# One queue for all transfers of the loop: loads, delayed stores and transposes issued by SyncE in a windowed-attention backward kernel

## The chip, the cores and the metric

The kernel runs on one core of one Trainium2 chip. The metric is device time in microseconds (us) of one execution. Five engines carry the work: TensorE (PE; its weight loads are shown as PEld), VectorE (DVE), ScalarE (ACT), GpSimd (POOL) and SyncE (SP). Transfers are issued by an engine's instruction stream and then carried out by the core's 16 DMA engines. In the profile, an issuing stream is shown as SPq, POOLq or ACTq.

## The reference

Forward and backward of attention in windows of 8 x 8 pixels over a 256 x 256 image with 384 channels, all in bf16:

```python
H = W = 256; C, win = 384, 8          # x and grad_out: (1, 256, 256, 384)
def forward(x, wqkv, wo):
    xw = windows_of(x)                 # 1024 windows, each 64 pixels x 384
    q, k, v = split(xw @ wqkv)         # wqkv: (384, 1152)
    p = softmax(einsum('bqc,bkc->bqk', q, k) * C ** -0.5)
    return image_of(einsum('bqk,bkc->bqc', p, v) @ wo)
out, vjp = jax.vjp(forward, x, wqkv, wo)
return out, *vjp(grad_out)             # out_0 = out, out_1 = dx, out_2 = dwqkv, out_3 = dwo
```

## The kernel before

**Tiling.** Two windows (128 pixels) make a pair of partition halves, and four pairs stacked in the image make a quad: 128 partitions x 4 x 384. The image is 128 quads. The kernel works with products of the weights (A from the q and k weights, B from the v and output weights) made once at the start, so a quad needs the transposed x and the transposed output gradient, their projections, scores, a softmax and its gradient, and sums for the weight gradients.

**The loop.** The loop at the end of the kernel runs i from -1 to 128. Each turn calls `step(c, b, a, ahead)`, which works on three quads in different stages: `a` = quad i+1 (projections), `b` = quad i (scores, softmax and the u and v products), `c` = quad i-1 (`attend`: the products with the probabilities, the outputs and dx). `filler` puts the weight-gradient sums of earlier quads, in groups of three, between these parts.

**Order.** The order in which instructions stand on each engine is written out by hand (`tc.manual_schedule` with all five engines). The framework only adds the semaphore waits. Each engine's stream runs in that order, and a waiting instruction holds back all that stands behind it.

**Transfers of one turn**, in the order in which SP's stream holds them:

1. `load_turn(sts[i + 2])`: two transposing transfers, dT<-dq and xT<-xq of quad i+2 (line 134), 12 blocks of 128 x 128 each.
2. `turn(b)`: PS<-ps of quad i (line 239), 4 blocks; it follows the last softmax step.
3. `load(ahead)`: four copies of x for quad i+3 (line 126), 96 KB each.
4. `to_tokens(a)`: tok<-zy of quad i+1 (line 171), 24 blocks; it follows the second `gather`.

POOL's stream holds four copies of the output gradient (dq, line 127) from `load`, and nine stores of the quad in `attend` (lines 298 to 305): four of 96 KB to out_0, three of 96 KB and two of 48 KB to out_1. Each store of `attend` stands right behind the evictions that make its data. The evicted outputs lie in tiles "o" and "d" of a pool with 8 buffers each, and a quad uses 4 of each.

**Consumers.** dT is first needed by `project(a, 0, ...)` of the following turn (pj<-dT, line 145), xT by `project(a, 1, ...)` of the same turn. PS is needed by `attend` of the following turn, and tok by `attend` one turn after that.

Of the kernel before, what the change touches and what calls it, by code (L numbers as in the profile page):

```python
# [22 lines left out]
def kernel(  # L23
# [21 lines left out]
    nc = tc.nc  # L45
# [28 lines left out]
    def fetch_weights():  # L74
        nc.sync.dma_start(out=w_sb[:, :, columns(2)], in_=w_in[:, :, columns(2)])
        nc.scalar.dma_start(out=wo_sb[:], in_=wo.rearrange("(m p) n -> p m n", p=P))
        for k in (0, 1):
            nc.scalar.dma_start(out=w_sb[:, :, columns(k)], in_=w_in[:, :, columns(k)])

    def warm_up(n):  # L80
        zero = B_sb[:].rearrange("p m c -> p (m c)")[:, 0:4 * P]
        nc.vector.memset(zero, 0.0)
        for i in range(n):
            pt = ring.tile([P, 4 * P], F32, tag="r", name="warm")
            nc.tensor.matmul(pt[:], lhsT=zero[:, 0:P], rhs=zero, start=True, stop=True)
# [25 lines left out]
    def weight_rest():  # L111
        weight_product(B_sb, wT[2], wo_sb, None)
        weight_product(AT_sb, wT[1], wT[0], scale)

    def windows(ap, st, first, count=2):
        row, col = st["at"]
        return ap[0, row + WIN * first:row + WIN * (first + count), col:col + WIN, :]

    LO, HI = slice(0, WT), slice(WT, P)
    OTHER = {0: HI, WT: LO}  # L120

    def load(st):
        st["xq"] = xq = grp.tile([P, QUAD, C], BF16, tag="xq", name="xq", bufs=2 * GQ + 4)
        st["dq"] = dq = qp.tile([P, QUAD, C], BF16, tag="dq", name="dq", bufs=6)
        for t in range(QUAD):
            nc.sync.dma_start(out=xq[:, t, :], in_=windows(x, st, 2 * t))
            nc.gpsimd.dma_start(out=dq[:, t, :], in_=windows(grad_out, st, 2 * t))  # L127

    def load_turn(st):
        st["xT"] = qp.tile([P, QUAD, CK, P], BF16, tag="xT", name="xT", bufs=3)  # L130
# [111 lines left out]
    def operand(st, n, t, h):  # L242
        if n in ("PT", "ST"):
            return st["PS"][h, t, int((n == "ST") == (h == LO)), :]
        if n in ("z", "y"):
            return st["tok"][h, int(n == "y"), :, t, :]
        return st[n][h, t, :]

    def attend(st, pair):
        if pair[0] == 0:  # L250
            st["Uq"] = grp.tile([P, QUAD, C], BF16, tag="Uq", name="Uq")
            st["Wq"] = grp.tile([P, QUAD, C], BF16, tag="Wq", name="Wq")

        def bank(name):
            return ring.tile([P, C], F32, tag="r", name=name)

        def slot(straight, crossed, start=False, stop=False):
            for h in (LO, HI):
                dst, lhs, rhs, t = straight
                products = [(h, dst[h, :], lhs, rhs, t, {"start": True, "stop": True})]  # L260
                lhs, rhs, t = crossed
                o = OTHER[h.start]
                dst = pd[int((t == t0) == (h == LO))]
                products.append((o, dst[o, :], lhs, rhs, t, {"start": start, "stop": stop}))
                for o, dst, lhs, rhs, t, flags in products if h == LO else products[::-1]:
                    nc.tensor.matmul(dst, lhsT=operand(st, lhs, t, h), rhs=operand(st, rhs, t, h), **flags)  # L266

        def keep(name, src):
            sb = ob.tile([P, C], BF16, tag=name, name=name)
            nc.scalar.copy(out=sb[:], in_=src[:])  # L270
            return sb

        t0, t1 = pair
        pw = {t: bank("pw") for t in pair}
        pu = {t0: bank("pu")}
        pd = [bank("pd") for outer in (0, 1)]
        po = {t0: bank("po")}
        pu[t1] = bank("pu")
        po[t1] = bank("po")
        slot((pw[t0], "Pb", "dq", t0), ("Pb", "z", t0), start=True)  # L280
        nc.scalar.copy(out=st["Wq"][:, t0, :], in_=pw[t0][:])  # L281
        slot((pw[t1], "Pb", "dq", t1), ("dS", "y", t0))
        nc.vector.tensor_copy(out=st["Wq"][:, t1, :], in_=pw[t1][:])
        slot((pu[t0], "ST", "xq", t0), ("Pb", "z", t1), start=True)
        nc.vector.tensor_copy(out=st["Uq"][:, t0, :], in_=pu[t0][:])
        slot((po[t0], "PT", "uq", t0), ("dS", "y", t1))
        o0 = keep("o", po[t0])
        slot((pu[t1], "ST", "xq", t1), ("ST", "vq", t0), stop=True)
        nc.vector.tensor_copy(out=st["Uq"][:, t1, :], in_=pu[t1][:])
        slot((po[t1], "PT", "uq", t1), ("ST", "vq", t1), stop=True)  # L290
        o1 = keep("o", po[t1])
        inner = keep("d", pd[0])
        if t0 == 0:
            st["mid"], st["rim"] = [ob.tile([P, C], BF16, tag="d", name="d") for k in range(2)]
        upper, lower = (st["rim"], st["mid"]) if t0 == 0 else (st["mid"], st["rim"])
        nc.scalar.copy(out=lower[LO, :], in_=pd[1][LO, :])
        (nc.scalar.copy if t0 else nc.vector.tensor_copy)(out=upper[HI, :], in_=pd[1][HI, :])
        nc.gpsimd.dma_start(out=windows(out_0, st, 2 * t0), in_=o0[:])  # L298
        nc.gpsimd.dma_start(out=windows(out_0, st, 2 * t1), in_=o1[:])
        nc.gpsimd.dma_start(out=windows(out_1, st, 2 * t0 + 1), in_=inner[:])  # L300
        if t0 == 0:
            nc.gpsimd.dma_start(out=windows(out_1, st, 0, 1), in_=st["rim"][HI, :])
        else:
            nc.gpsimd.dma_start(out=windows(out_1, st, 3), in_=st["mid"][:])
            nc.gpsimd.dma_start(out=windows(out_1, st, 7, 1), in_=st["rim"][LO, :])

    fill = []

# [17 lines left out]
    def filler(n):  # L326
        while n and fill:
            try:
                next(fill[0])
                n -= 1  # L330
            except StopIteration:
                fill.pop(0)

    def step(c, b, a, ahead):


        def on(st):
            return (lambda f, *r: f(st, *r)) if st is not None else (lambda f, *r: None)
        C_, B, A = on(c), on(b), on(a)
        B(scores)  # L340
        B(soft, 0)
        if b is not None and c is None:
            weight_rest()
        B(uv, 0, 0)
        B(uv, 0, 1)
        B(soft, 1)
        B(uv, 1, 0)
        B(uv, 1, 1)
        B(soft, 2)
        B(soft, 3)  # L350
        B(uv, 2, 0)
        B(uv, 2, 1)
        B(uv, 3, 0)
        B(uv, 3, 1)
        B(soft, 4)
        for mo in range(CK):
            A(project, 0, mo)
        B(soft, 5)
        B(turn)
        if ahead is not None:  # L360
            load(ahead)
        filler(1)
        C_(attend, (0, 1))
        A(gather, 0)
        for mo in range(CK):
            A(project, 1, mo)
        A(gather, 1)
        A(to_tokens)
        filler(1)
        C_(attend, (2, 3))  # L370

    G_ON_PE, X_ON_PE = 4, 1
    EV = {"z": "AAA", "y": "AAA", "u": "AAAA", "v": "AAAA", "o": "AAAA", "U": "DDDD", "W": "DDDD", "d": "AAAA"}
    quads = [(row, col) for row in range(0, H, 2 * WIN * QUAD) for col in range(0, W, WIN)]
    sts = [{"at": q, "i": i} for i, q in enumerate(quads)]
    n = len(sts)
    AHEAD = 3
# [40 lines left out]
    with tc.manual_schedule(engines=MANUAL):  # L418
        fetch_weights()
        warm_up(9)  # L420
        load(sts[0])
        make_identity(nc, ident[:])
        load(sts[1])
        load(sts[2])
        load_turn(sts[0])
        load_turn(sts[1])
        turn_blocks(wT[2], w_sb, 2 * CK)
        weight_product(BT_sb, wo_sb, wT[2], None)
        turn_on_pe(sts[0], "dq", "dT")
        turn_on_pe(sts[0], "xq", "xT")  # L430
        turn_blocks(wT[0], w_sb, 0)
        turn_blocks(wT[1], w_sb, CK)
        weight_product(A_sb, wT[0], wT[1], scale)
        nc.vector.memset(GF_acc[:], 0.0)
        held = []
        last = None
        get = lambda i: sts[i] if 0 <= i < n else None
        for i in range(-1, n + 1):
            if 0 <= i < n - 2:
                load_turn(sts[i + 2])  # L440
            step(get(i - 1), get(i), get(i + 1), get(i + AHEAD) if i >= 0 else None)
            if 0 < i + 2 < G_ON_PE:
                turn_on_pe(sts[i + 2], "dq", "dT")
            if i == 1:
                turn_blocks(woT_sb, wo_sb)
            if i > 0:
                held.append(sts[i - 1])
                sts[i - 1] = None
            if held and i == n:
                last = gf_group(held, True)  # L450
            elif len(held) == GQ:
                fill.append(gf_group(held))
                held = []
        filler(1 << 30)
        weight_gradients(last)
# [30 lines left out]
```

## Time and profile before

| what | value |
|---|---|
| runs | 1941.6, 1948.11, 1948.42 us; median 1948.11 us |
| profiled execution | span 1942.8 us from first to last instruction |
| TensorE clock granted, mean | 0.999 |
| busy share of the span | PE 99%, ACT 80%, DVE 75%, POOL 46% |
| DMA queues, share of 16 engines' span | q1 (from SP) 79.0%, q0 (from POOL) 30.8% |
| HBM read and written | 101.84 MB each |

The busy shares count work on data. Instructions that issue transfers are not counted as busy on SP and ACT, so SP has no row in the table of engines, and its stream has to be read from the timeline. The two queue shares may overlap in time on the same DMA engine, so their sum can pass 100%.

### The profile page before, as it was taken

What the parts mean: (1) busy time and instruction counts of PE and PEld (TensorE: products, weight loads), DVE (VectorE), ACT (ScalarE), POOL (GpSimd) and SP (SyncE); (2) the same over time, 40 slices, a digit from 0 to 9 for tenths busy, and PEclk for the clock granted to TensorE, in tenths of its full rate; (3) what the DMA queues carried; (4) which work ended last, traced back from release to release, by engine and by line L of the source; (5) the groups of instructions that cost most, each with busy time, mean ns of one, the idle gap of its engine ahead of it and who ended that gap; (6) DMA issues with size and microseconds to landing.
All of it is one profiled execution on the core that took longest, in us unless ns stands there. A gap on an engine that the chain in (4) does not pass through costs nothing.

```text
span 1942.8 us, 48771 instructions
## 1 busy us (share of the span) xinstructions
PE 1926.6 (99%) x17859; PEld 1076.9 (55%) x17859; DVE 1458.9 (75%) x3244; ACT 1546.3 (80%) x3613; POOL 895.2 (46%) x1670
## 2 busy tenths in 40 slices
PE   9999999999999999999999999999999999999999
PEld 5555555555555555555555555555555555555555
DVE  6777767777777777777777777777777777777776
ACT  7878878778777878887787878788887878887775
POOL 3445444444444445444444454454444445444432
PEclk9999999999999999999999999999999999999999
DMA  8999999999999999999999999999999999999994
GB/s 186 220 222 227 224 204 222 224 217 224 223 221 226 226 220 223 226 221 220 219 228 222 221 219 229 221 225 217 230 218 228 224 219 220 226 224 219 222 195 109
DMA packets 1017584, 423.21 MB, mean 218 GB/s; under 512 B 899584, under 2 KB 992768, under 8 KB 1017344
## 3 DMA queue, kind: packets, MB, share of 16 engines
q1 hardware_dynamic: 935984, 267.85, 79.0%
q0 software_dynamic: 79872, 151.17, 30.8%
q8 instruction: 140, 2.29, 0.5%
q10 hardware_dynamic: 1488, 1.08, 0.2%
q14 instruction: 100, 0.82, 0.1%
HBM read 101.84 MB, written 101.84 MB: 105 GB/s over the span
## 4 chain that ended last, share of the span: by engine, by line
PE 94%; ACT 2%; DMA 2%; DVE 1%; issue 0%; SPq 0%; POOL 0%; ACTq 0%; POOLq 0%
PE pj L145 49%; PE pg L145 25%; PE pw L266 6%; PE sd L145 5%; PE pu L266 4%; PE po L266 4%; DMA PS<-ps 1%; DMA dT<-dq 1%; PE pd L266 1%; ACT uq L235 0%; ACT vq L235 0%; DMA dq<-in_grad_out_dram 0%; ACT yz L159 0%; PE pe L385 0%; SPq L134 0%
## 5 line engine op out<-in xcount | busy, mean ns | idle before, releaser
L298 POOL DMA_DIRECT2D out_dram<-o x256 | 137.7, 538 | 936.8 <-ACT o L270 915.8
L145 PEld LDWEIGHTS <-xq 128*128 128x128 bf16 x3072 | 300.0, 98 | 226.4 <-issue 2.0
L145 PEld LDWEIGHTS <-xT 128*128 128x128 bf16 x3072 | 291.6, 98 | 182.7
L145 PE MATMUL pj<-B_sb,xT 128*128 128x384 bf16 x1536 | 333.5, 326 | 0.0
L145 PE MATMUL pj<-AT_sb,xT 128*128 128x384 bf16 x1536 | 333.3, 326 | 0.0
L127 POOL DMA_DIRECT2D dq<-in_grad_out_dram x512 | 271.9, 547 | 40.4 <-DMA out_dram<-o 17.6
L281 ACT CAST Wq<-pw 128x384 bf16<-128x384 f32 x256 | 123.0, 480 | 200.1 <-PE pw L266 200.0
L145 PE MATMUL pj<-dT,BT_sb 128*128 128x512 bf16 x1152 | 271.3, 381 | 5.1 <-DMA dT<-dq 5.1
L145 PE MATMUL pg<-Uq,xq 128*128 128x384 bf16 x1536 | 270.4, 326 | 0.5 <-DVE GF_acc L321 0.5
L145 PE MATMUL pj<-xT,A_sb 128*128 128x512 bf16 x1152 | 270.8, 380 | 0.0
L145 PE MATMUL pg<-Wq,xq 128*128 128x384 bf16 x1536 | 270.4, 326 | 0.0
L321 DVE TENSOR_TENSOR GF_acc<-pg,GF_acc 128x384 f32<-128x384 f32 x258 | 143.9, 558 | 152.8 <-PE pg L145 152.7
L235 ACT CAST uq<-pj 128x384 bf16<-128x384 f32 x512 | 249.9, 488 | 7.3 <-PE pj L145 1.0
L235 ACT CAST vq<-pj 128x384 bf16<-128x384 f32 x512 | 255.1, 498 | 0.1
L270 ACT CAST o<-po 128x384 bf16<-128x384 f32 x512 | 220.9, 484 | 5.1 <-PE po L266 2.4
L211 ACT COPY ps<-Pb 64x256 bf16<-64x256 bf16 x256 | 103.2, 403 | 149.7 <-DVE Pb L208 148.2
L159 ACT CAST yz<-pj 128x512 bf16<-128x512 f32 x384 | 206.7, 644 | 2.1 <-PE pj L145 2.0
L161 ACT CAST yz<-pj 128x512 bf16<-128x512 f32 x384 | 200.8, 607 | 0.2
L145 PEld LDWEIGHTS <-BT_sb 128*128 128x128 bf16 x1152 | 112.4, 98 | 129.8 <-DMA dT<-dq 7.0
L145 PEld LDWEIGHTS <-A_sb 128*128 128x128 bf16 x1152 | 102.3, 98 | 139.9 <-issue 33.6
L167 DVE COPY zy<-yz 128x1536 bf16<-128x1536 bf16 x256 | 143.4, 560 | 46.3 <-ACT yz L161 39.8
L266 PE MATMUL pd<-tok,Pb 64*64 64x384 bf16 x1024 | 173.3, 335 | 0.0
(89 smaller groups left out, 3376.1 us busy)
## 6 DMA issues: line engine op xcount, KB each, us to landing
xq<-in_x_dram SPq DMA_DIRECT2D x512, 96.0 KB, 4.2
dq<-in_grad_out_dram POOLq DMA_DIRECT2D x512, 96.0 KB, 4.0
out_dram<-o POOLq DMA_DIRECT2D x512, 96.0 KB, 4.0
out_dram<-d POOLq DMA_DIRECT2D x384, 96.0 KB, 4.2
out_dram<-d POOLq DMA_DIRECT2D x256, 48.0 KB, 4.3
tok<-zy SPq DMA_TRANSPOSE x128, 7.6
PS<-ps SPq DMA_TRANSPOSE x128, 4.7
xT<-xq SPq DMA_TRANSPOSE x127, 6.3
```

The costliest lines, as they stand in the source:

```text
L127: nc.gpsimd.dma_start(out=dq[:, t, :], in_=windows(grad_out, st, 2 * t))
L145: nc.tensor.matmul(out, lhsT=lhsT, rhs=rhs, start=start, stop=stop)
L159: ENG[EV["z"][mo]](out=yz[:, mo, :, 0:4:3, :], in_=pj[:])
L161: ENG[EV["y"][mo]](out=yz[:, mo, :, 1:3, :], in_=pj[:])
L167: nc.vector.tensor_copy(out=st["zy"][:, kind, :, :, :, :], in_=src)
L211: nc.scalar.copy(out=ps[h, :, w, :], in_=Pb[h, :, :])
L235: cp(out=dst[:, t, :], in_=pj[:])
L266: nc.tensor.matmul(dst, lhsT=operand(st, lhs, t, h), rhs=operand(st, rhs, t, h), **flags)
L270: nc.scalar.copy(out=sb[:], in_=src[:])
L281: nc.scalar.copy(out=st["Wq"][:, t0, :], in_=pw[t0][:])
L298: nc.gpsimd.dma_start(out=windows(out_0, st, 2 * t0), in_=o0[:])
L321: nc.vector.tensor_tensor(out=GF_acc[:, f, ma, :], in0=pw[:], in1=GF_acc[:, f, ma, :], op=ALU.add)
```

## The change

All transfers of the loop go to SP's stream. The four dq copies of `load` stand between the x copies. The nine stores of a quad are no longer issued in `attend`: `attend` only notes them, and a new function `store` issues them one turn later, behind the loads and ahead of `to_tokens`. `step` therefore gets a fourth quad, `d` = quad i-2. The last quad's nine stores stay on POOL, directly behind its two `attend` calls. Arithmetic, tiles and buffer counts are the same.

```diff
@@ load
             nc.sync.dma_start(out=xq[:, t, :], in_=windows(x, st, 2 * t))
-            nc.gpsimd.dma_start(out=dq[:, t, :], in_=windows(grad_out, st, 2 * t))
+            nc.sync.dma_start(out=dq[:, t, :], in_=windows(grad_out, st, 2 * t))
@@ attend, end
-        nc.gpsimd.dma_start(out=windows(out_0, st, 2 * t0), in_=o0[:])
-        nc.gpsimd.dma_start(out=windows(out_0, st, 2 * t1), in_=o1[:])
-        nc.gpsimd.dma_start(out=windows(out_1, st, 2 * t0 + 1), in_=inner[:])
+        kept = [(out_0, 2 * t0, 2, o0[:]), (out_0, 2 * t1, 2, o1[:]), (out_1, 2 * t0 + 1, 2, inner[:])]
         if t0 == 0:
-            nc.gpsimd.dma_start(out=windows(out_1, st, 0, 1), in_=st["rim"][HI, :])
+            kept.append((out_1, 0, 1, st["rim"][HI, :]))
         else:
-            nc.gpsimd.dma_start(out=windows(out_1, st, 3), in_=st["mid"][:])
-            nc.gpsimd.dma_start(out=windows(out_1, st, 7, 1), in_=st["rim"][LO, :])
+            kept += [(out_1, 3, 2, st["mid"][:]), (out_1, 7, 1, st["rim"][LO, :])]
+        st.setdefault("kept", []).extend(kept)
+
+    def store(st, queue):
+        for ap, first, count, sb in st.pop("kept", ()):
+            queue.dma_start(out=windows(ap, st, first, count), in_=sb)
@@ step
-    def step(c, b, a, ahead):
+    def step(d, c, b, a, ahead):
...
         if ahead is not None:
             load(ahead)
+        if d is not None:
+            store(d, nc.sync)
         filler(1)
         C_(attend, (0, 1))
+        if c is not None and c["i"] == n - 1:
+            store(c, nc.gpsimd)
...
         C_(attend, (2, 3))
+        if c is not None and c["i"] == n - 1:
+            store(c, nc.gpsimd)
@@ the loop
-            step(get(i - 1), get(i), get(i + 1), get(i + AHEAD) if i >= 0 else None)
+            step(get(i - 2), get(i - 1), get(i), get(i + 1), get(i + AHEAD) if i >= 0 else None)
...
-                sts[i - 1] = None
+            if i > 1:
+                sts[i - 2] = None
```

The order in which SP's stream then holds one turn's 21 transfers: dT, xT, PS, eight copies in (x and dq in turn), nine stores of quad i-2, tok. The framework shares eight completion semaphores among SP's transfers in turn, so that nearly every transfer waits for the one issued eight before it.

## The prediction

> **What bounds the kernel now.** I read the page's engine table first, then the chain that ended last, then the timeline of SP's stream, which the engine table leaves out, and last the answers on single lines of issues.
>
> ```profile
> PE 1926.6 (99%) x17859; PEld 1076.9 (55%) x17859; DVE 1458.9 (75%) x3244; ACT 1546.3 (80%) x3613; POOL 895.2 (46%) x1670
> PE 94%; ACT 2%; DMA 2%; DVE 1%; issue 0%; SPq 0%; POOL 0%; ACTq 0%; POOLq 0%
> ```
>
> PE is busy for 99% of the span and carries 94% of the chain. So PE sets the pace: from the `project` products on A_sb at 900.63 us to the same place one turn later at 915.42 us is 14.8 us. DMA ends 2% of the chain, some 39 us; that is about all that better transfers could give back. The page seems to leave SP out of the matter. The timeline of SP's stream does not (start, duration, instruction; "idle before" would follow in brackets):
>
> ```profile
> 901.58 1.45 SPq L134 DMA_TRANSPOSE dT<-dq  x1
> 903.21 3.15 SPq L134 DMA_TRANSPOSE xT<-xq  x1
> 906.51 1.26 SPq L239 DMA_TRANSPOSE PS<-ps  x1
> 907.83 2.63 SPq L126 DMA_DIRECT2D xq<-in_x_dram  x4
> 910.56 4.94 SPq L171 DMA_TRANSPOSE tok<-zy  x1
> 915.73 1.42 SPq L134 DMA_TRANSPOSE dT<-dq  x1
> 917.66 3.44 SPq L134 DMA_TRANSPOSE xT<-xq  x1
> 921.26 1.19 SPq L239 DMA_TRANSPOSE PS<-ps  x1
> 922.51 2.79 SPq L126 DMA_DIRECT2D xq<-in_x_dram  x4
> 925.41 5.28 SPq L171 DMA_TRANSPOSE tok<-zy  x1
> ```
>
> Add start and duration in any line and you are within 0.06 to 0.51 us of the next start. The first turn holds 1.45 + 3.15 + 1.26 + 2.63 + 4.94 = 13.4 us of issuing in 14.15 us, and what remains is a chain of short waits that were already fulfilled. SP is as full as PE, with eight transfers in a turn. It runs late as well: tok goes out at 910.56, though the last gather of its data ended at 904.06 on DVE. PE does not suffer, because dT, issued at 901.58, is needed at 910.34 and lands a median 5.9 us after issue, some 2.9 us early. So SP can fall behind by about 3 us once. After that each microsecond that SP's turn is longer than PE's is paid in every turn.
>
> **The change part by part.** The prices of issues come from these rows (minimum, median and maximum in ns):
>
> ```profile
> L126 SPq DMA_DIRECT2D xq<-in_x_dram x512: 536/600/1881, 1.2 to 1879.5; - x171
> L171 SPq DMA_TRANSPOSE tok<-zy x128: 3607/4768/6755, 18.9 to 1900.3; - x128
> L134 SPq DMA_TRANSPOSE xT<-xq x127: 1432/2944/5716, 12.9 to 1887.1; - x127
> L134 SPq DMA_TRANSPOSE dT<-dq x124: 1422/1578/3497, 49.2 to 1884.3; - x124
> L239 SPq DMA_TRANSPOSE PS<-ps x128: 1188/1426/2388, 28.9 to 1909.9; - x128
> ```
>
> *dq copies, four in a turn, from POOL to SP.* They have the shape of the x copies. Four of those take 2.53 to 2.79 us, 0.63 to 0.70 each with the gap behind; I take 0.64. That is not queueing behind POOL's traffic: at 30.09 us, when POOL was issuing nothing, four took 2.52. Price: 4 x 0.64 = 2.6 us.
>
> *Stores, nine in a turn, from POOL to SP.* The trace shows no windowed store from SP. From below there are SP's plain final stores, 0.34 us (dw, line 416) to 0.40 (dw, line 407). From above there is the windowed load, 0.64 with its gap. The windowed store has the load's two patterns with the sides exchanged (16 x 8 x 384 in the image, 128 x 384 on chip), and on POOL loads and stores cost alike (547 and 538 ns), so I take 0.64: 9 x 0.64 = 5.8 us. With 0.40 it is 3.6. Waiting for data costs nothing here: the stores are of quad i-2, evicted a turn earlier.
>
> Here two statements of the Trainium skill speak for the change doing no harm. Its page "DMA: Bandwidth & Descriptors", section "Issuing engines are not separate DMA queues", says that transfers of all issuers share the same 16 engines and that issuing from several saves only the sequencers' issue time, usually small against the transfer. The rows above already show issue time filling SP's turn; by the rule as worded the time would stay at 1948. The same page, under "Anatomy of one DMA", puts the sequencer's dispatch at about 50 ns; by that the 13 copies would cost 0.7 us a turn, against the 600 ns apiece in the row.
>
> *Transposes.* Their data and count stay. Now POOL's packets share the DMA engines with them (79.0% and 30.8%), which stretches them: in quiet places tok took 4.33 (at 32.72), 3.91 (at 1880.20) and 3.63 us (at 1900.33) against a median of 4.77, and xT 1.45 (at 22.64) and 1.43 (at 37.27) against 2.94. In the new order the copies' packets stand ahead in the same queue, but over a longer turn. I take values near the quiet ones: tok 4.0, dT 1.58, xT 1.8, PS 1.3, and 0.1 each for gaps: 9.1 us. Bounds: 8.05 with all four minima, 11.1 with all four medians. This is the change's only gain, about 2 to 3 us a turn.
>
> *Sum for SP's turn:* 17 x 0.64 + 9.1 = 20.0 us, against 14.8 of PE. The cover that hid SP is gone after the first turns; what is late next is dT, then PS, and PE waits some 5 us in every turn.
>
> *Semaphores in turn.* Each transfer waits for the eighth before it. Eight copies take 5.1 us to issue and x copies land a median 4.2 us after issue; behind tok (7.6 us to landing) stand dT, xT, PS and four or more copies. So these waits cost nothing if landings stay as they are; a landing of 6 us would add about 0.1 us a copy, 1.9 us a turn, and I leave that to the range.
>
> *POOL, buffers, DMA engines.* POOL loses 1655 of its 1664 loop transfers (512 dq and 1152 stores); POOL is on 0% of the chain, worth nothing. The output tiles are held a turn longer: 8 buffers are two quads, and the store two quads back leaves before SP's next tok, so ACT waits for it at most within PE's new idle time. If that cover were gone, `attend` would stall by a store's landing, about 4 us. The DMA engines: packet records of the trace show 18 ns per 256-byte transpose packet and 36 ns per 768-byte copy packet undisturbed; 416 and 17 x 8 of them per engine make 12.4 us a turn, below both 14.8 and 20.0, so the engines are no bound.
>
> *The whole.* Before, the first PS goes out at 28.85 us and the last at 1909.9, 32.9 us before the end. I put the first at 32, since 24 loads now stand ahead in SP's stream instead of 12 and the first transposed dq comes some 3 us later. Between lie 127 turns x 20.0 = 2540 us, less what the first and last turns lack (two turns' loads and stores, three dT, two xT: 30 us). 32 + 2510 + 33 = 2575 us of span. The median of the runs is 5.3 us above the profiled span: 2580 us.
>
> **The rivals.**
> 1. *Windowed stores are as cheap as SP's plain ones* (0.40 instead of 0.64): 125 x 9 x 0.24 = 270 us less, 2310 us. For it: the source is a plain tile. Against it: source and image pattern differ as in the load, and that is what tells 0.60 from 0.34.
> 2. *The transposes stay as slow as their medians of before*, since copies now stand right ahead of them in one queue: 2.0 us a turn more, 254 us, 2835 us. For it: tok was slower behind four copies (4.33) than alone (3.63). Against it: the DMA engines have 12.4 us of work in 20.
> 3. *Not slower: an issue's duration is mostly waiting for room, which the relieved DMA engines give back.* Price: with the smallest issue of the page, 0.34 for all 17 copies, and transposes at 1.2 + 1.4 + 1.4 + 1.8 (PS, dT, xT, and tok by the step from 4 to 12 blocks continued to 24), a turn is 11.6 us. It decides once SP's turn is below PE's 14.8; then PE bounds, and of the 39 us of DMA in the chain perhaps half goes: 1930 to 1950 us. Against it: no x copy of 512 took under 536 ns, 17 of which are 9.1 us, and with the minima of the transposes that is 17.2.
>
> That the stores do not move is no case: the diff and the built order of SP's stream show all of them there.
>
> **How the numbers follow.** The forecast, 2580 us, has 0.72; rival 1 has 0.10, rival 2 has 0.14, rival 3 has 0.04. The forecast's own bounds are 2440 (minima of the transposes) to 2700 (half of rival 2). The range takes in most of rivals 1 and 2: 2320 to 2835. A measurement of this kernel can tell about 0.5% from no change, so of rival 3 half falls within and half below: faster 0.02, same 0.02, slower 0.96.
>
> **What would show each step right or wrong.** Right: SP's timeline has back-to-back issues of 20 us a turn, the windowed stores near 0.6 us, xT under 2.2 us; PE's share falls to about 75%; the longest PE waits name dT and PS; the chain names SPq and DMA instead of PE. Wrong in size: stores at 0.4 us, transposes at 4.8 and 2.9, or gaps between SP's issues, which would be the eight semaphores. Wrong in kind: SP's stream with idle time before PS or tok while PE keeps 99%.

## The result, and the profile after

| | before | after |
|---|---|---|
| median of the runs | 1946.96 us | 2659.95 us |
| profiled span | 1942.8 us | 2655.1 us |
| ratio | 1 | 1.3674, 95% interval 1.3646 to 1.3703 |
| PE busy, share of the span | 1926.6 us, 99% | 2216.6 us, 83% |
| TensorE clock granted, mean | 0.999 | 0.918 |

The changed kernel is slower by 36.7%; the forecast was 2580 us, 32% over before, in a range from 2320 to 2835. Of the ten executions in the experiment "The delay alone" below, one took 3354.51 us at a granted clock of 0.592; its ratio is taken without that one. The page of the changed kernel, its table of engines and the chain that ended last (by engine, then by line):

```profile
PE 2216.6 (83%) x17859; PEld 1167.9 (44%) x17859; DVE 1458.5 (55%) x3244; ACT 1599.5 (60%) x3613; POOL 5.7 (0%) x15
...
SPq 44%; PE 19%; ACT 14%; DMA 11%; DVE 6%; issue 6%; DVEq 0%; ACTq 0%
SPq L307 17%; SPq L127 12%; SPq L126 12%; DMA out_dram<-d 11%; PE pj L145 10%; ACT yz L161 6%; PE sd L145 5%; SPq L239 3%; ACT vq L235 3%; DVE GF_acc L323 3%; ACT uq L235 3%; DVE zy L167 2%; PE po L266 2%; ACT ex L200 1%; PE pg L145 1%
```

The chain has moved from PE (94% before) to SP's stream: the stores (L307), the dq copies (L127) and the x copies (L126) hold 41% of it. No engine in the first line is near its limit any more, and SP has no entry there. One turn of SP's timeline, in the columns used before:

```profile
1319.56 1.45 SPq L134 DMA_TRANSPOSE dT<-dq  x1
1321.06 1.79 SPq L134 DMA_TRANSPOSE xT<-xq  x1
...
1329.01 0.60 SPq L127 DMA_DIRECT2D dq<-in_grad_out_dram  x1
1329.65 1.25 SPq L307 DMA_DIRECT2D out_dram<-o  x2
1330.94 1.97 SPq L307 DMA_DIRECT2D out_dram<-d  x2
1332.95 1.20 SPq L307 DMA_DIRECT2D out_dram<-o  x2
1334.19 1.91 SPq L307 DMA_DIRECT2D out_dram<-d  x3
1336.20 3.68 SPq L171 DMA_TRANSPOSE tok<-zy  x1
1340.00 1.45 SPq L134 DMA_TRANSPOSE dT<-dq  x1
```

From dT to dT is 20.4 us, and again each line begins where the one above it ends. The prices, in the answers on single lines (minimum, median and maximum in ns):

```profile
L307 SPq DMA_DIRECT2D out_dram<-d x635: 555/598/2056, 65.3 to 2636.3; - x159
L307 SPq DMA_DIRECT2D out_dram<-o x508: 542/596/1807, 64.0 to 2633.6; - x170
L171 SPq DMA_TRANSPOSE tok<-zy x128: 3563/3652/4587, 20.6 to 2619.1; - x128
L134 SPq DMA_TRANSPOSE xT<-xq x127: 1432/1919/3726, 18.8 to 2597.9; - x127
L134 SPq DMA_TRANSPOSE dT<-dq x124: 1340/1453/2213, 52.9 to 2596.4; - x124
L239 SPq DMA_TRANSPOSE PS<-ps x128: 1188/1425/2032, 28.8 to 2622.8; - x128
```

A windowed store costs SP 0.60 us like a windowed load. The transposes became shorter (medians): tok 3.65 us against 4.77, xT 1.92 against 2.94. So the gain was there, and thirteen issues outweighed it.

### The profile page after: what moved, and what is told of

The parts are those of the page before. It is cut to its first block, busy times and chain, and to the rows that moved or that the text cites. A ratio compares the mean times of both kernels' runs of the same rounds, so it can differ in the third digit from the quotient of the medians.

```text
span 2655.1 us, 46744 instructions
## 1 busy us (share of the span) xinstructions
PE 2216.6 (83%) x17859; PEld 1167.9 (44%) x17859; DVE 1458.5 (55%) x3244; ACT 1599.5 (60%) x3613; POOL 5.7 (0%) x15
## 4 chain that ended last, share of the span: by engine, by line
SPq 44%; PE 19%; ACT 14%; DMA 11%; DVE 6%; issue 6%; DVEq 0%; ACTq 0%
SPq L307 17%; SPq L127 12%; SPq L126 12%; DMA out_dram<-d 11%; PE pj L145 10%; ACT yz L161 6%; PE sd L145 5%; SPq L239 3%; ACT vq L235 3%; DVE GF_acc L323 3%; ACT uq L235 3%; DVE zy L167 2%; PE po L266 2%; ACT ex L200 1%; PE pg L145 1%
## 5 line engine op out<-in xcount | busy, mean ns | idle before, releaser
L297 DVE CAST d<-pd 64x384 bf16<-64x384 f32 x128 | 71.8, 561 | 734.3 <-DMA out_dram<-d 435.4
L145 PEld LDWEIGHTS <-xT 128*128 128x128 bf16 x3072 | 328.7, 110 | 249.2 <-issue 104.8
L145 PE MATMUL pj<-B_sb,xT 128*128 128x384 bf16 x1536 | 396.9, 374 | 0.0
L145 PE MATMUL pj<-AT_sb,xT 128*128 128x384 bf16 x1536 | 379.3, 361 | 0.0
L266 PE MATMUL pw<-dq,Pb 64*64 64x384 bf16 x1024 | 162.7, 345 | 196.8 <-ACT yz L161 196.3
L296 ACT CAST d<-pd 64x384 bf16<-64x384 f32 x256 | 121.9, 476 | 267.6 <-DMA out_dram<-d 267.6
L266 PE MATMUL po<-uq,PS 64*64 64x384 bf16 x1024 | 188.5, 349 | 97.5 <-DVE GF_acc L323 96.5
L266 PEld LDWEIGHTS <-PS 64*64 64x64 bf16 x3072 | 140.0, 107 | 199.4 <-issue 175.7
L266 PE MATMUL pu<-xq,PS 64*64 64x384 bf16 x1024 | 183.1, 341 | 13.3 <-ACT yz L161 0.7
L204 DVE TENSOR_REDUCE rs<-ex 128x4 f32<-128x256 f32 x128 | 53.7, 420 | 240.4 <-ACT ex L200 240.4
```

The lines of the kernel that those rows point to most:

```text
L145: nc.tensor.matmul(out, lhsT=lhsT, rhs=rhs, start=start, stop=stop)
```

## The experiments

Four theories were put to the test. **A**: the sum of issue durations on SP's stream is the turn. **B**: the later stores hold the output tiles, ACT and DVE wait for their landings, and this sets the turn. **C**: the work of the DMA engines in one queue sets it. **D**: not SP's stream is full but something behind it that SP shares with ACT, a generator of the transfers' descriptors. A fifth, **F**, is about the size alone. For B there is this in the waits of the changed kernel (engine, line, who was waited for: us in total, times, longest):

```profile
DVE d L297 <- DMA out_dram<-d: 435.4, 74, 7.7
...
ACT o L270 <- DMA out_dram<-o: 297.2, 146, 4.4
ACT d L296 <- DMA out_dram<-d: 267.6, 124, 3.6
```

That is 1000 us of waits for stores, more than the 713 us that the kernel lost.

**The delay alone.** From the kernel before, stores noted and issued a turn later, but on POOL, and dq on POOL (against the changed kernel):

```diff
-            nc.sync.dma_start(out=dq[:, t, :], in_=windows(grad_out, st, 2 * t))
+            nc.gpsimd.dma_start(out=dq[:, t, :], in_=windows(grad_out, st, 2 * t))
...
-            store(d, nc.sync)
+            store(d, nc.gpsimd)
```

> The kernel before, with only the delay of the change: the stores of a quad are issued one turn later, on POOL, and the dq copies stay on POOL. Theory A: no issue is added to SP; within 0.5% of before, 1937 to 1957 us. Theory B (output tiles held a turn longer hold up ACT, DVE and with them PE): slower by several per cent, 2050 us or more.

Measured: 1939.94 us, ratio 0.9988 (0.9974 to 1.0001). Holding the output tiles a turn longer costs nothing by itself.

**Stores ahead of the loads.**

```diff
-        if ahead is not None:
-            load(ahead)
         if d is not None:
             store(d, nc.sync)
+        if ahead is not None:
+            load(ahead)
```

> The changed kernel with a turn's nine stores ahead of its eight loads instead of behind them, so that output tiles come free some 5 us earlier in the turn; the same 21 transfers on SP. Theory A: same sum of issues, 2645 to 2675 us, while the waits of ACT and DVE for stores shrink. Theory B: those waits are in the path, so it gets faster by 3 us a turn or so, 2280 us.

Measured: 2684.8 us, ratio 1.3821 (1.3798 to 1.3845), some 1% slower than the change. Its waits for stores, and ahead of them PE's longest wait for a transfer, are these:

```profile
PE pj L145 <- DMA dT<-dq: 502.5, 121, 6.2
...
DVE d L297 <- DMA out_dram<-d: 41.4, 24, 3.5
...
ACT d L296 <- DMA out_dram<-d: 40.8, 38, 2.7
```

1000 us of waits became 82 us among the 60 longest, and the time did not fall. B has fallen: those waits lay in the time that PE, ACT and DVE had to spare anyway. Once they were gone, another wait stood there: PE now waits 502 us for dT, the transfer that the prediction had named as the next to be late. SP's turn is 20.6 us against 20.4. Its issue durations add up to only 15 us more over the run: tok, now behind loads instead of stores, has a mean of 4.10 us against 3.69, and xT 1.79 against 2.30.

**dq back on POOL, or the stores back on POOL.** The first undoes the dq line in the changed kernel; the second makes that change alone in the kernel before.

```diff
-            nc.sync.dma_start(out=dq[:, t, :], in_=windows(grad_out, st, 2 * t))      # in the changed kernel
+            nc.gpsimd.dma_start(out=dq[:, t, :], in_=windows(grad_out, st, 2 * t))
@@ the second
-            nc.gpsimd.dma_start(out=dq[:, t, :], in_=windows(grad_out, st, 2 * t))    # in the kernel before
+            nc.sync.dma_start(out=dq[:, t, :], in_=windows(grad_out, st, 2 * t))
```

> The changed kernel, with the four dq copies of a turn back on POOL (17 transfers a turn on SP instead of 21). Theory A (the sum of issue times on SP's stream sets the turn): in the profile after, SP's turn is 9.3 us of transposes with their gaps and 17 copies at 0.67; four copies less make 18.0 us, 2316 us in all. If POOL's packets again stretch the transposes in proportion (four of the 13 transfers that cost 2.75 us a turn before), 18.9 us and 2420. Theory B (the landings of the delayed stores, for which ACT and DVE wait over 1000 us in total, set the turn): the stores stay where they are, so 2600 us or more.

> The kernel before, with the four dq copies alone moved to SP; the stores stay on POOL right behind their evictions. Theory A: 8 copies at 0.67 and 9.3 us of transposes make 14.7 us, just under PE's 14.8, if POOL's stores do not stretch the transposes; with nine of the thirteen POOL transfers left, 1.9 us more: 16.6 us and 2170 us. So between 1950 and 2170, nearer the upper end. Theory B: the stores are where they were, so 1950.

Measured, one run each: 2509.23 us and 2281.9 us. Both lie between before and after, and both outside what A had given (2316 to 2420, and 1950 to 2170). The first fits B's 2600 no better, the second is far from B's 1950. What A had wrong was not the sum but one term, the transposes. With the stores back on POOL:

```profile
L171 SPq DMA_TRANSPOSE tok<-zy x128: 3594/4576/6391, 20.5 to 2237.7; - x128
L134 SPq DMA_TRANSPOSE xT<-xq x127: 1432/3014/4381, 18.7 to 2225.8; - x127
L134 SPq DMA_TRANSPOSE dT<-dq x124: 1442/2564/3637, 54.4 to 2222.4; - x124
```

tok and xT are as long as before and dT is longer (2.56 us against 1.58), although only nine of the thirteen transfers that shared the DMA engines with them are left on POOL. I had taken the stretch in proportion. With dq on POOL it is xT that is stretched, to a median of 3.00 us. In the chain of the kernel with the stores back, the transfer that the prediction had named as the next to be late appears:

```profile
PE pj L145 34%; PE pg L145 21%; DMA dT<-dq 20%; PE pw L266 4%; PE sd L145 4%; PE pu L266 3%; PE po L266 3%; DMA PS<-ps 3%; ACT vq L235 1%; ACT uq L235 1%; PE pd L266 0%; ACT o L270 0%; ACT ex L200 0%; DVE rs L204 0%; ACT d L297 0%
```

The 20% are the time of dT's transfers from issue to landing; of these PE itself waited about half (us in total, times, longest):

```profile
PE pj L145 <- DMA dT<-dq: 221.9, 73, 5.2
```

By engine this chain has PE at 71%, DMA at 24% and SPq at 0%. But SP's stream is full in this run too: its mean gap is 0.05 us before a copy and 0.11 to 0.19 before a transpose. So I take it that dT lands late because SP issues it late.

**No stores in the loop.**

```diff
         if d is not None:
-            store(d, nc.sync)
+            d.pop("kept")
```

> The changed kernel without the stores of the loop (the outputs of all quads but the last are not written); loads and transposes stay on SP. Theory A: SP's turn is 9.3 + 8 x 0.67 = 14.7 us, at PE's own 14.8: 1945 to 1990 us, PE again near 99%. Against the run with the stores on POOL, this one tells what their packets cost the transposes. Theory B: also about 1950, since nothing is waited for. Theory C: 1950 as well.

Measured, one run: 1948.7 us, with PE at 99% again and these transposes:

```profile
L171 SPq DMA_TRANSPOSE tok<-zy x128: 3602/3908/4662, 21.1 to 1904.3; - x128
L134 SPq DMA_TRANSPOSE xT<-xq x127: 1434/1750/3149, 19.3 to 1892.2; - x127
```

Eight copies and four transposes on SP just fit beside PE. With the same twelve issues and the nine stores on POOL it was 333 us more. That is what the nine stores from POOL cost SP's transposes, 2.6 us a turn.

**Half the bytes, or twice the issues.** The first writes half of each store (half of both outputs stays unwritten); the second splits each store into two of half the rows.

```diff
-            queue.dma_start(out=windows(ap, st, first, count), in_=sb)
+            half = slice(0, WT) if count == 2 else slice(0, WT // 2)
...                                                            # dst: the upper half of the rows
+            queue.dma_start(out=dst, in_=sb[half, :])
@@ the second
-            queue.dma_start(out=windows(ap, st, first, count), in_=sb)
...                                                            # row, col, rows: the place, and half of the rows
+            for k in range(2):
+                queue.dma_start(out=ap[0, row + k * rows:row + (k + 1) * rows, col:col + WIN, :],
+                                in_=sb[k * rows * WIN:(k + 1) * rows * WIN, :])
```

> The changed kernel with the same nine stores a turn on SP, each of half its bytes (half of both outputs is not written). Theory A: an issue costs the same for half the bytes (the 48 KB stores took 0.63 us, the 96 KB ones 0.60), so the time stays: 2660 us, or up to 35 us more if smaller shapes cost 0.63. Theory C (the DMA engines' work in one queue sets the turn): nine stores carry about 2.6 us of packet time per engine and turn at 36 ns a packet; half of it gone makes 1.3 us a turn, 2495 us.

> The changed kernel with every store of a turn split into two of half the rows: 18 issues instead of nine, the same bytes, all outputs written. Theory A (the turn is the sum of issues on SP): 125 turns x 9 more issues at 0.67 us = 754 us more, 3410 us. Theory C (the DMA engines' work): same bytes and packets, so 2660.

Measured, one run each: 2677.3 us with half the bytes, 3448.92 us with twice the issues. Half the bytes bring nothing. Nine more issues a turn of the same bytes cost 789 us, which is 0.69 us for each of the 1143 that the trace has more. C has fallen: what counts is how many transfers are issued, not what they carry (24 to 96 KB each here).

**dq on ACT.** In the changed kernel:

```diff
-            nc.sync.dma_start(out=dq[:, t, :], in_=windows(grad_out, st, 2 * t))
+            nc.scalar.dma_start(out=dq[:, t, :], in_=windows(grad_out, st, 2 * t))
```

> The changed kernel with the four dq copies of a turn issued by ACT. Theory A: what is full is SP's stream, so 4 x 0.67 us leave its turn: 18.0 us and 2316 us, if ACT, with 60% busy, has room for four issues and does not come to wait for SP's transfers, with which it shares the eight semaphores. Theory D (what is full is one descriptor generator behind both streams): it stays at 2650.

Measured, one run: 2446.02 us. Four issues fewer on SP bring 214 us, so D has fallen; SP's copies kept their median of 0.597 us. It is 130 us short of A's figure, and the waits of this run show what came in:

```profile
ACT Wq L281 <- DMA xq<-in_x_dram: 374.4, 96, 5.8
PE pj L145 <- ACT Wq L281: 353.8, 121, 5.6
```

ACT's dq copies wait on semaphores that they share with SP's transfers, and ACT's evictions stand behind them. PE then waits for ACT, PS gets its data later, and SP has a gap before PS, 1.0 us in the mean against 0.2, which is some 100 of the 130 us.

**All copies on POOL.** The opposite of the change, in the kernel before:

```diff
-            nc.sync.dma_start(out=xq[:, t, :], in_=windows(x, st, 2 * t))
+            nc.gpsimd.dma_start(out=xq[:, t, :], in_=windows(x, st, 2 * t))
```

> The opposite of the change: the kernel before, with the x copies moved to POOL too, so that SP issues the four transposes alone. Theory A: SP's turn falls from 14.8 to some 11.9 us of issues, SP runs ahead of PE instead of behind it, and PE, at 14.8 us a turn, sets the time alone: 1930 to 1945 us, faster by 0.1 to 0.9%. If POOL's 17 copies (9.3 us of issues a turn) hold the loads behind stores that wait for data, it could be slower by up to 1%.

Measured: 1960.66 us, ratio 1.0100 (1.0081 to 1.0119): slower by 1%. SP issues the four transposes alone and is still nearly full (the profiled execution is the slowest of the seven, 1977.56 us):

```profile
1014.20 3.06 SPq L134 DMA_TRANSPOSE xT<-xq  x1
1017.42 1.19 SPq L239 DMA_TRANSPOSE PS<-ps  x1
1018.71 7.37 SPq L171 DMA_TRANSPOSE tok<-zy  x1
```

tok takes 7.4 us here, 6.5 in the median, against 4.8 before. Four x copies taken off SP saved it 3 us a turn, and their packets, now in POOL's queue, gave 3.3 us back in the transposes. My fear for this run, loads held behind stores that wait, is not ruled out as a part of it: in 20 turns SP was idle for 0.6 to 6.2 us before dT, 58 us in all. Once, for example, tok's issue ended at 475.98 us and dT went out at 481.74; POOL had issued the last dq copy of that quad at 471.34. How the 1% divides between the two stays open.

**The sum, over all of these.** Mean durations and gaps of SP's issues from the traces, and the mean distance from one PS to the next:

| kernel | copies on SP, a turn | x mean with gap, us | transposes with gaps, us | sum, us | turn measured, us |
|---|---|---|---|---|---|
| before | 4 | 0.74 | 12.1 | 15.0 | 14.8 |
| all copies on POOL | 0 | | 15.3 | 15.3 | 15.1 |
| no stores | 8 | 0.67 | 9.6 | 15.0 | 14.8 |
| stores on POOL | 8 | 0.68 | 12.3 | 17.7 | 17.5 |
| dq on POOL | 13 | 0.68 | 10.8 | 19.6 | 19.2 |
| after | 17 | 0.67 | 9.3 | 20.7 | 20.4 |
| twice the stores | 26 | 0.68 | 9.4 | 27.0 | 26.6 |

The sum is 0.2 to 0.4 us above the turn throughout, since the first and last turns lack issues. As the gaps are counted in, the sum has to meet the turn, so this agreement proves nothing by itself. That SP has hardly any idle time is told by the gaps: 0.05 us in the mean before a copy and 0.05 to 0.28 before a transpose, save 0.67 before dT with all copies on POOL. What the table tells is that a copy's price holds from 8 to 26 copies, while the transposes' price rises with what POOL issues: 9.3 to 9.6 us with nothing, 10.8 with four transfers a turn, 12.1 to 12.3 with 13 and nine, 15.3 with 17.

**Where the last 3% came from.** The turn was 20.4 us where 20.0 were forecast for a full one. The trace's packet records have 139 packets of 16 KB in the instruction queue q8, 1.1 us each in the mean. xT has a mean of 2.94 us where such a packet overlaps it or ended less than 1 us ahead of it (55 times), 1.82 elsewhere (72); copies have 0.86 and 0.60. Of the 52 xT over 2.3 us, 51 are among those beside a packet. Over all issues the excess is some 120 us. That is a coincidence in time, not yet a cause. F says that the packet lengthens the issue beside it.

```diff
+    spare = const.tile([P, 2], F32)
...
     def step(d, c, b, a, ahead):
+        for k in range(128):
+            nc.gpsimd.memset(spare[0:1, k % 2:k % 2 + 1], 0.0)
```

> The changed kernel with 128 memsets of one element a turn on the idle POOL, which feed nothing, so that more of the 16 KB instruction-fetch packets run beside SP's issues. In the changed kernel's trace, issues that such a packet overlaps are longer (xT 2.94 us against 1.82, copies 0.8 to 0.9 against 0.60), in all some 120 us for 139 packets. Theory F (the fetches lengthen them): 16,500 more instructions are some 50 to 65 more packets, so 40 to 60 us more, 2700 to 2720 us. Rival (a coincidence, or POOL's fetches do not matter): 2645 to 2675 us.

Measured: 2667.01 us, ratio 1.3721 (1.3688 to 1.3754), not told apart from the change. The page shows why this was no test of those packets (queue, kind: packets, MB, share):

```profile
q8 instruction: 139, 2.28, 0.3%
q14 instruction: 215, 1.76, 0.2%
```

POOL's instructions came in queue 14, where 85 packets had been, and queue 8 stayed at 139. F as I had put it, for any instruction fetch, is wrong. PE's own instructions were the next to try:

```diff
         C_(attend, (2, 3))
+        pt = ring.tile([P, 4 * P], F32, tag="r", name="spare")
+        for k in range(40):                                   # the control: range(10), 512 columns
+            nc.tensor.matmul(pt[:, 0:16], lhsT=ident[:], rhs=w_sb[:, 0, 0:16], start=True, stop=True)
```

> The changed kernel with 40 short products a turn added on PE behind the second attend (weights of 128 x 128, 16 columns, nothing reads the result), some 10,400 more PE instructions. The 139 packets of 16 KB in queue 8 fit PE's 35,700 instructions at 64 bytes, so there should be some 41 more of them. Theory F (such a packet lengthens SP's issue that it overlaps, about 120 us for 139 packets, 0.9 us each): 35 us more than the changed kernel, 2690 to 2700 us, and more long xT. Rival (they only coincide, or PE's added time counts): the same as the run with ten long products. PE has some 4 us of idle time in a turn, and 40 pairs take 2 to 4.

> The control: ten products of 512 columns a turn in the same place, about the same time on PE and a quarter of the instructions, so some 10 more fetch packets. Theory F: 9 us more than the changed kernel, 2660 to 2680 us, and some 25 us under the run with 40 short ones. Rival: no difference between the two runs beyond 0.3%.

Measured: 2683.63 us with 40 short products (2679.23 to 2686.99) and 2664.22 with ten long ones (2663.54 to 2665.61), 19 us apart, where F had 25; the first is below F's own 2690 to 2700. Queue 8 had 180 packets in the first and 149 in the second. xT with the short ones, then in the control:

```profile
L134 SPq DMA_TRANSPOSE xT<-xq x127: 1438/2755/3370, 18.7 to 2622.7; - x127
```

```profile
L134 SPq DMA_TRANSPOSE xT<-xq x127: 1432/1831/3533, 18.8 to 2598.8; - x127
```

31 more packets came with 24 us more of issue durations on SP (2497.5 against 2473.5), and long xT became the common case. This supports F for PE's fetches. So does the run with the stores first: there only 8 of the 127 xT had such a packet beside them, and xT's mean was 1.79 us (2.66 for these 8, 1.73 for the others). It doesn't prove F: the kernels also differ in what PE does and when, and how a fetch packet would hold SP's issue was not tried.

## Why the prediction was right

**The bound.** The step that carried the forecast was that SP's stream, absent from the table of engines, was as full as PE. It was shown by taking issues off SP and adding some: without the nine stores the turn falls to PE's 14.8 us, with the four dq copies elsewhere 18.7 (ACT) and 19.2 (POOL), with nine more stores 26.6, against 20.4. Neither bytes (C), nor tiles held longer (B), nor a shared generator (D) explain that.

**Stores at the price of windowed loads.** Right: medians of 0.596 and 0.598 us. Rival 1, with the 0.40 us of the plain stores, is out; the plain stores of this kernel still cost 0.35 to 0.41.

**Transposes near their quiet values.** Right in the sum, 9.3 us with gaps against 9.1 in the forecast, and rival 2 is out. Single terms were off: tok 3.69 us in the mean where 4.0 were taken, xT 2.30 where 1.8 were taken. That these two errors nearly cancel in the sum was luck.

**The size.** The forecast was 80 us low. The copies had 0.67 us with their gap instead of 0.64, 0.5 us a turn; xT had 0.5 more, tok 0.3 less, and the rest is in dT, PS and gaps. That makes 0.6 to 0.7 us a turn, near 80 us. The medians were near the forecast (copies 0.597 without their gap, xT 1.92 against 1.8); the means are pulled up by long issues, most of them beside fetch packets. I had priced from medians and quiet rows, and a sum needs means.

**The eight semaphores.** Rightly left at nothing on SP: PS, issued at 1302.33, had landed by 1305.08, and the copy that waits for it began at 1308.31. They cost something only where ACT shared them.

**What was late next.** Wrong for this kernel: its longest waits are ACT's and DVE's for the stores' landings, and PE waits for ACT (196 and 112 us in all) and hardly for dT (9.8 us). PE did wait for dT in the runs with the stores first (502 us), the stores back on POOL (222) and dq back on POOL (124). The forecast had named the wait for the stores and put it inside idle time at no cost, and that was right, as the run with the stores first shows. PE was idle for 3.4 us a turn where some 5 were given. Its share was given as 75%; it is 83%: the same 17859 products took 2216.6 us instead of 1926.6, with a mean clock of 0.918 against 0.999.

**Rival 3**, that issues shrink once the DMA engines are relieved, has fallen for copies (0.600 to 0.597 us) and was the whole gain in transposes.

**Issue time by the written rule.** The page "DMA: Bandwidth & Descriptors" of the Trainium skill, under "Issuing engines are not separate DMA queues", counts the issue time as usually small; here nine more issues a turn cost 789 us, and the measurement decides. The dispatch of about 50 ns that the prediction took from the same page stands there in an account of transfers issued by GpSimd, so it was no price for SP's; the row with 600 ns was. That all issuers' transfers run on the same DMA engines and interleave, as the section on issuing engines says, agrees with this case: POOL's stores cost SP's transposes 2.6 us a turn.

## What to carry to other kernels

Before you move transfers to one queue, add up the issue durations of that engine's stream over one turn of the loop, from the timeline: the table of busy engines does not count them, and a stream whose lines follow each other without gaps is a bound for whatever is added to it, even beside a PE at 99%. Price a moved transfer by an issue of the same access pattern, take means and not medians, and count transfers rather than bytes. Then ask in both directions: a transfer left in another queue costs this stream no issue, but it may stretch the transposes. Here that was as much for the four x copies (3.3 us a turn against 3.0 of issues), and less than half for the nine stores (2.6 against 6.0).

## What the runs showed of the hardware that was not expected

- A transposing transfer holds the issuing stream longer when another engine issues transfers beside it: tok took 3.62 to 3.97 us (medians of the runs) with nothing on POOL, 4.58 with nine transfers a turn there, 4.77 with 13, and 6.48 with 17.
- An instruction-fetch packet of 16 KB beside an issue on SP went with 1.1 us more for xT (2.94 against 1.82 us in the changed kernel).
- PE slowed down after short idle times. In the changed kernel, after waits of 2.2, 1.8 and 0.7 us within one turn, the same 24 products took 1.46 us, in the kernel before 0.87. The first line is of before, the second of after:

```profile
905.73 0.87 PE L145 MATMUL sd<-xT,yz 128*128 128x64 bf16 x24
```

```profile
1319.64 1.46 PE L145 MATMUL sd<-xT,yz 128*128 128x64 bf16 x24
```

The granted clock was 0.50 from 1317.7 to 1324.5 us, and 0.918 in the mean of the run: 90 stretches at half speed, 435 us together, although PE was never idle for more than 3.39 us at a time. The Trainium skill, "TensorE: Matmul & The Clock Gate", "Part 1: The HAM clock gate", says that the clock is halved after an idle window of about 3.4 us; the waits inside this turn were shorter each. It cost no time that the runs show: the control with ten long products had 0.952 and took 2664 us, against 2660.
